# Halving the attention products of chunk 0 in a transformer block, with a new order of work on all engines

## The chip, the cores and the metric

The kernel runs on one core of one Trainium2 chip. A core has a matrix engine (TensorE, PE in the profile), a vector engine (VectorE, DVE), an engine for activations and copies (ScalarE, ACT), a general one (GpSimd, POOL) and one that issues DMAs (SyncE, SP). They run side by side, each through its own list of instructions, and wait for each other by semaphores. Sixteen DMA engines move data for all of them. The metric is the device time of one execution in microseconds (us); less is better.

## The reference

A transformer block on 2048 rows of width 512, in bf16. Attention has 32 heads of width 16; each row looks at 8 earlier rows, 0, 2, ..., 14 back. The MLP has width 1376 and a gated ReLU.

```
qkv = layernorm(x) @ wqkv                    # q, k, v: 32 heads x 16
logits[s, w] = q[s] . k[s - 2*w] * 16**-0.5  # w = 0..7; rows before the first are masked
attn = softmax(logits over w)
o[s] = sum over w of attn[s, w] * v[s - 2*w]
h = x + o @ wo
n = layernorm(h)
out = h + (relu(n @ W_gate) * (n @ W_up)) @ W_down
```

## The kernel before

**Tiling.** The rows are cut into four chunks of 512 (four blocks of 128 rows each). Activations stand transposed in SBUF: the width on the 128 partitions in four tiles (a tile holds 4 of each head's 16 values for all 32 heads), the chunk's 512 rows along the free dimension. kT and vT hold k and v of all rows, so a shift by 2w rows is only another offset.

**The steps of a chunk**, with the names that the code gives them:

- Layer norm of x: statistics on VectorE (`xst`, `xag`, L431, L434), Ln and Exp on ScalarE (L444, L448), the normalised rows on VectorE (`xxn`, L466), then the transposition. It runs on TensorE for chunks 0 to 2 (`xtp`, L495), with copies out of PSUM by ScalarE (`xte`, L511) or VectorE (`xtv`, L509), and by DMA transposes from SyncE for chunk 3 (`xtd`, L484, one for each block of 128 rows).
- Projections (`qkv`, L536): twelve of four matmuls each; the first four of chunk 0 in two halves of the rows (`qka`, `qkc`). ScalarE copies the results to q, kT and vT (`qe`, L544).
- Products q*k (`pr`, L583): one VectorE instruction multiplies two tiles of q by four shifts of k, 128x4096 elements; two for each half of the shifts. TensorE sums them over the head's width by 16 matmuls (`sc`, L589). ScalarE takes the exponentials (`ex`, L619), in chunk 0 VectorE sets the masked ones to zero (`mk`, L622). `den` (L639) forms the denominators, L642 and L645 their reciprocals.
- The weights are spread over the head's width, in chunks 0 and 1 by TensorE (`bc`, L689) and ScalarE's copies (`be`, L695), in chunks 2 and 3 by broadcasting DMAs from SyncE (`bd`, L679).
- Products weight*v (`mu`, L710): one instruction for a tile takes all eight shifts, 128x4096. In chunks 0 to 2 an accumulating DMA that GpSimd issues adds the upper four shifts to the lower four (`ta`, L742, 512 KB each); VectorE adds the rest (`tree`, L713). In chunk 0 the reciprocal denominator is multiplied in at the end (`om`, L717).
- Output projection and residual (`wo`, L762 and L765, with L771 or L773), the second layer norm (L420, L412), its transposition (`htp`, L495 and `hte`, L511, or `htd`, L484), the MLP (`mm`, L800, copies L804 and L807, product `gu`, L820), the down projection (`dn`, L837), the last sum (L848) and the output DMA (`os`, L854).

**What sets the order.** Every step above is registered in a `Plan` with its engine, an assumed duration, the steps it depends on and the buffers it takes. `Plan.order` then simulates the engines: each engine takes its own steps in the order of the table `RANK`, a number for each step, and the buffer that a step gets, and so whom it waits for, follows from that simulated order. The instructions are emitted in the resulting order. TensorE's results share 8 PSUM banks, the products 5 buffers `big`, the MLP products 7 buffers `gT`.

The DMAs of the inputs are issued ahead of the plan, in `setup` (L290 to L321): x of chunk 0, wqk_sb, x of chunk 1, wv_sb, the rest of x, then wo, W_up, W_gate and W_down. 44 warm-up matmuls (L385) and two groups of eight (`fill`, L393) keep TensorE busy until the first weights land.

Of the kernel before, what the change touches and what calls it, by code (L numbers as in the profile page):

```python
# [19 lines left out]
    24, 32, 27, 17, 20, 22, 25, 26, 30, 35, 36, 29, 34, 37, 39, 41, 43, 47, 23, 28,  # L20
    31, 33, 38, 45, 48, 42, 59, 65, 40, 51, 55, 46, 56, 60, 49, 52, 57, 73, 76, 61,
    79, 67, 72, 71, 74, 80, 106, 88, 95, 75, 96, 91, 104, 103, 93, 113, 119, 127, 70, 85,
    94, 98, 102, 172, 175, 185, 130, 134, 136, 149, 152, 105, 108, 110, 114, 111, 188, 197, 223, 226,
    231, 179, 190, 217, 221, 228, 171, 180, 208, 211, 219, 158, 169, 195, 207, 210, 245, 252, 236, 241,
    239, 244, 243, 249, 256, 260, 247, 253, 246, 250, 255, 261, 266, 269, 276, 281, 275, 279, 285, 278,
    283, 282, 286, 291, 310, 315, 326, 330, 293, 322, 314, 324, 348, 329, 361, 337, 345, 339, 342, 346,
    350, 365, 333, 358, 349, 354, 340, 352, 353, 356, 363, 323, 328, 316, 321, 302, 313, 308, 312, 332,
    364, 373, 366, 370, 306, 379, 369, 394, 405, 359, 393, 355, 380, 402, 404, 421, 442, 445, 395, 424,
    453, 574, 374, 413, 447, 450, 389, 409, 436, 473, 50, 53, 44, 62, 54, 64, 58, 63, 66, 69,
    77, 90, 78, 83, 92, 81, 87, 82, 86, 89, 118, 129, 157, 170, 124, 196, 164, 178, 97, 101,  # L30
    166, 182, 100, 116, 150, 159, 132, 186, 107, 176, 137, 156, 109, 126, 200, 213, 218, 237, 232, 240,
    251, 258, 262, 264, 274, 284, 287, 288, 296, 294, 292, 298, 300, 307, 305, 309, 303, 318, 327, 360,
    367, 311, 319, 341, 347, 336, 343, 372, 377, 325, 334, 368, 375, 382, 385, 384, 388, 381, 383, 386,
    398, 390, 392, 397, 400, 387, 396, 401, 403, 406, 407, 408, 411, 414, 417, 410, 418, 412, 419, 422,
    457, 467, 434, 484, 477, 480, 461, 481, 491, 472, 475, 429, 466, 449, 460, 441, 476, 478, 433, 435,
    454, 458, 446, 451, 439, 443, 462, 474, 503, 427, 431, 469, 486, 502, 505, 508, 493, 512, 465, 525,
    507, 518, 511, 521, 529, 497, 516, 504, 513, 520, 531, 552, 569, 572, 524, 541, 666, 707, 514, 533,
    537, 540, 536, 539, 580, 708, 112, 120, 99, 121, 68, 84, 115, 122, 125, 133, 144, 163, 147, 160,
    165, 142, 148, 135, 145, 161, 229, 234, 233, 242, 187, 202, 177, 199, 174, 183, 192, 194, 184, 189,
    206, 235, 212, 215, 181, 191, 193, 205, 214, 238, 289, 265, 297, 317, 248, 257, 290, 301, 331, 335,  # L40
    338, 357, 344, 362, 371, 415, 425, 456, 459, 423, 432, 464, 470, 430, 438, 468, 471, 391, 399, 448,
    455, 479, 483, 490, 495, 485, 492, 482, 488, 487, 489, 499, 501, 494, 496, 498, 506, 509, 515, 519,
    522, 526, 528, 527, 534, 517, 532, 596, 601, 562, 594, 565, 589, 558, 591, 604, 544, 553, 542, 551,
    555, 560, 548, 550, 570, 549, 557, 546, 556, 579, 583, 568, 573, 586, 599, 608, 609, 614, 571, 576,
    603, 611, 618, 617, 626, 613, 629, 588, 631, 606, 627, 632, 620, 624, 585, 616, 635, 639, 662, 668,
    672, 623, 641, 643, 677, 628, 636, 638, 675, 634, 637, 645, 647, 117, 141, 128, 139, 131, 140, 123,
    138, 143, 146, 155, 162, 153, 167, 168, 173, 151, 154, 204, 225, 254, 268, 273, 299, 259, 270, 209,
    227, 216, 220, 267, 280, 224, 230, 201, 222, 198, 203, 263, 272, 271, 277, 304, 295, 320, 376, 378,
    351, 416, 420, 426, 428, 437, 444, 440, 463, 452, 530, 535, 543, 561, 500, 510, 523, 566, 547, 554,
    564, 567, 538, 545, 559, 563, 593, 597, 575, 578, 577, 581, 582, 587, 600, 602, 590, 598, 584, 595,  # L50
    592, 605, 607, 610, 619, 622, 615, 625, 621, 633, 612, 630, 657, 689, 683, 687, 667, 673, 671, 680,
    692, 640, 656, 658, 660, 648, 654, 650, 661, 664, 676, 679, 644, 652, 678, 682, 655, 663, 684, 649,
    651, 653, 670, 642, 646, 665, 669, 674, 694, 696, 685, 693, 659, 690, 681, 686, 698, 691, 699, 688,
    697, 701, 710, 714, 717, 719, 705, 709, 711, 715, 695, 702, 704, 706, 700, 703, 712, 713, 716, 718,
    720, 721,
# [36 lines left out]
class Plan:  # L92


    HOP = 0.06

# [19 lines left out]
    def order(self):  # L116
# [14 lines left out]
        while left:  # L131
# [37 lines left out]
            if op.dq:  # L169
                at = max(t + op.dur + op.dq[0], free.get("DQ", 0.0)) + op.dq[1]  # L170
                free["DQ"] = at
                op.done = at + op.lat
# [19 lines left out]
def kernel(  # L192
# [23 lines left out]
    PRE = ()  # L216
    NAB = 0
# [127 lines left out]
    DAL = 5.5  # L345
    TDD, TDL = 1.25, 1.5
# [13 lines left out]
    HG = ([[0, 1, 2, 3]],) * 4  # L360

# [12 lines left out]
    def load(t):  # L374
        return add(None, "LD", 0.0, None, lat=t)

    xload = [[load(t) for t in (3.5, 3.7, 4.1, 4.35)]] + [[load(t)] * BPC for t in (9.15, 13.2, 15.4)]
    wload = {n: load(t) for n, t in
             (("q", 7.78), ("k", 7.78), ("v", 10.6), ("o", 17.1), ("u", 20.5), ("g", 24.0), ("d", 28.5))}
# [139 lines left out]
    for tk in range(NCK):  # L519
# [49 lines left out]
        for hf in range(2):  # L569
            sc, ex = Buf(at_s), Buf(ex_s)  # L570
            scd, prd = [], []
            for t in range(0, NT, 2):
                pb = Buf(big_s)

                def f_pr(t=t, hf=hf, pb=pb, qT=qT, s0=s0):
                    kb = kT[:, t:t + 2, PADL + s0 - 4 * hf * DIL: PADL + s0 - 4 * hf * DIL + CS]
                    ka = [list(y) for y in kb.ap]
                    k4 = bass.AP(tensor=kb.tensor, offset=kb.offset,
                                 ap=[ka[0], ka[1], [-DIL, 4], ka[2]])
                    qb = qT.t[:, t:t + 2, :]  # L580
                    qa = [list(y) for y in qb.ap]
                    q4 = bass.AP(tensor=qb.tensor, offset=qb.offset, ap=[qa[0], qa[1], [0, 4], qa[2]])
                    V.tensor_tensor(out=pb.t[:].rearrange("p (t w) s -> p t w s", t=2),  # L583
                                    in0=q4, in1=k4, op=ALU.mult)

                def f_sc(t=t, sc=sc, pb=pb):
                    for u in range(2):
                        for g in range(4):
                            nc.tensor.matmul(sc.t[g * HB:(g + 1) * HB, :], lhsT=sel[:],  # L589
                                             rhs=pb.t[:, 4 * u + g, :], start=(t + u == 0),  # L590
                                             stop=(t + u == NT - 1), tile_position=(0, g * HB))

                a = add(("pr%d" % hf, tk), "DVE", D40, f_pr, [d[k] for k in (t, t + 1) for d in (qd, kd, kp)],
                        apr, take=[pb], use=[qT], lat=DL)
                prd.append((a, pb, f_sc))
            if (tk, hf) in PRE:
# [72 lines left out]
        for w0 in range(0, W, BCN):  # L669
            hf = w0 // 4  # L670
            if (tk, hf) in BCD:
                for eng, q in (("SP", nc.sync), ("ACT", nc.scalar), ("POOL", nc.gpsimd)):
# [4 lines left out]
                    def f_bd(ws=ws, q=q, w0=w0, ab=ab, ex=exs[hf]):  # L677
                        for w in ws:
# [3 lines left out]
                                   take=[ab], use=[exs[hf]], lat=0.77, dq=(0.75 - 0.5 * (len(ws) - 1), 0.5 * len(ws))))  # L682
# [19 lines left out]
        for t in range(NT):  # L702
# [13 lines left out]
            def f_om(t=t, mt=mt, rc=rc, OT=OT):  # L716
                V.tensor_tensor(out=OT.t[:, t, :], in0=mt.t[:, 0, :], in1=rc.t[:], op=ALU.mult)  # L717

            m = add(("mu%d" % t, tk), "DVE", D40, f_mu, abd + [vd[t], kdone.get(("v", tk - 1, t))], tpr,
                    take=[mt], use=[ab], lat=DL)  # L720
# [17 lines left out]
            for n, du in ((4, D20), (2, D10), (1, D2)):  # L738
                f = lambda n=n, mt=mt, f=f_a: f(n, mt)
                if n == 4 and (tk, t) in DACC:  # L740
                    def f_da(mt=mt):
                        nc.gpsimd.dma_start(mt.t[:, 0:4, :], mt.t[:, 4:8, :], accum_op=ALU.add)  # L742

                    m = add(("ta%d" % t, tk), "POOL", 1.0, f_da, [m], tpr, use=[mt], lat=1.1, dq=(0.75, 2.74))
                    continue
                if n == 1 and tk in EARLY:
                    oev[t] = add(("tree%d" % t, tk), "DVE", du, f_al, [m], tpr, take=[OT], use=[mt], lat=DL)
                else:
                    m = add(("tree%d" % t, tk), "DVE", du, f, [m], tpr, use=[mt], lat=0.11)
# [39 lines left out]
        for f0 in range(0, NFT, 2):  # L789
# [3 lines left out]
            for ft in fts:  # L793
# [4 lines left out]
                def f_mm(w_sb, mm, ft=ft, fs=fs, hnT=hnT):  # L798
                    for dt in range(NT):
                        nc.tensor.matmul(mm.t[:fs, :], lhsT=w_sb[:, dt, ft * P: ft * P + fs],  # L800
                                         rhs=hnT.t[:, dt, :], start=(dt == 0), stop=(dt == NT - 1))
# [4 lines left out]
                def f_ge(gm=gm, gr=gr, fs=fs, i=ft - f0):  # L806
                    nc.scalar.activation(out=gr.t[:fs, i, :], in_=gm.t[:fs, :], func=ACT.Relu)  # L807

                a = add(("mm%d" % (f0 // 2), tk), "PE", 4 * MM, lambda f=f_mm, um=um: f(wu_sb, um), hev + [wload["u"]], pr,
                        take=[um], use=[hnT], lat=PEL)  # L810
                b = add(("ue%d" % (f0 // 2), tk), "ACT", A5, f_ue, [a], pr - 200, take=[ub], use=[um], lat=AL)
                c = add(("mm%d" % (f0 // 2), tk), "PE", 4 * MM, lambda f=f_mm, gm=gm: f(wg_sb, gm), hev + [wload["g"]], pr,
                        take=[gm], use=[hnT], lat=PEL)
# [93 lines left out]
```

## Time and profile before

| | us |
|---|---|
| median of three runs | 200.72 (200.63 to 201.4) |
| the profiled execution | 201.23 |
| its span, from first to last instruction | 199.5 |
| TensorE busy | 191.6 |
| VectorE busy | 152.6 |
| ScalarE busy | 115.0 |

"Busy" is the time in which an engine has an instruction at work. Matmuls overlap in the array, so their starts say more than their durations: two of 512 columns follow each other after 0.216 us, though one is listed with 0.379 us. The same goes for VectorE, where an instruction starts some 0.08 us before the one ahead of it ends. Between one group's share of busy time and the kernel's time stands the chain of work: the profile follows it back from the last instruction, at each step to what released it. The waits list names for each engine what ended its idle time. A view of the DMA queues gives the packets that each moved in a stretch of time: q1 carries what SyncE issues, q0 what GpSimd issues.

### The profile page before, as it was taken

What the parts mean: (1) busy time and instruction counts of PE and PEld (TensorE: products, weight loads), DVE (VectorE), ACT (ScalarE), POOL (GpSimd) and SP (SyncE); (2) the same over time, 40 slices, a digit from 0 to 9 for tenths busy, and PEclk for the clock granted to TensorE, in tenths of its full rate; (3) what the DMA queues carried; (4) which work ended last, traced back from release to release, by engine and by line L of the source; (5) the groups of instructions that cost most, each with busy time, mean ns of one, the idle gap of its engine ahead of it and who ended that gap; (6) DMA issues with size and microseconds to landing.
All of it is one profiled execution on the core that took longest, in us unless ns stands there. A gap on an engine that the chain in (4) does not pass through costs nothing.

```text
span 199.5 us, 2918 instructions
## 1 busy us (share of the span) xinstructions
PE 191.6 (96%) x1080; PEld 95.7 (48%) x1099; DVE 152.6 (77%) x239; ACT 115.0 (58%) x240; POOL 12.6 (6%) x28
## 2 busy tenths in 40 slices
PE   8599999999999999999999999999999999999994
PEld 8385445554445344444444444444444444444542
DVE  6669999999999999998899859999964423032332
ACT  3455899881999987663844557701439620456500
POOL 4000000330000004100113000000000000000000
PEclk9999999999999999999999999999999999999999
DMA  6959981897000008985269970140010130102022
GB/s 166 327 185 324 412 283 32 156 192 148 3 0 0 3 0 157 190 165 123 39 118 196 208 204 2 26 85 20 3 53 0 26 79 0 31 0 79 0 79 79
DMA packets 19981, 20.92 MB, mean 105 GB/s; under 512 B 8608, under 2 KB 16768, under 8 KB 19968
## 3 DMA queue, kind: packets, MB, share of 16 engines
q1 hardware_dynamic: 17520, 13.60, 23.0%
q0 software_dynamic: 1728, 6.29, 16.8%
q10 hardware_dynamic: 720, 0.85, 1.6%
q8 instruction: 8, 0.13, 0.3%
q14 instruction: 5, 0.04, 0.1%
HBM read 8.42 MB, written 2.10 MB: 53 GB/s over the span
## 4 chain that ended last, share of the span: by engine, by line
PE 91%; DMA 4%; ACT 2%; issue 1%; SPq 1%; DVE 0%
PE bank L800 37%; PE bank L536 21%; PE bank L837 19%; PE bank L762 7%; DMA wqk_sb<-in_A_wqkv_dram 4%; PE bank L589 3%; PE bank L495 2%; ACT big L695 1%; PE bank L639 1%; ACT quad L511 1%; PE bank L765 0%; SPq L292 0%; PE bank L689 0%; ACT quad L544 0%; SPq L294 0%
## 5 line engine op out<-in xcount | busy, mean ns | idle before, releaser
L800 PE MATMUL bank<-quad,wu_sb 128*128 128x512 bf16 (+1 forms) x170 | 42.7, 379 | 0.7 <-ACT quad L511 0.3
L800 PE MATMUL bank<-quad,wg_sb 128*128 128x512 bf16 (+1 forms) x173 | 41.6, 379 | 0.1
L837 PE MATMUL bank<-wd_sb,gT 128*128 128x512 bf16 (+3 forms) x184 | 39.4, 366 | 0.2
L807 ACT ACTIVATE gr<-bank 128x512 bf16<-128x512 f32 (+1 forms) x44 | 25.3, 601 | 23.3 <-PE bank L800 21.8
L804 ACT CAST up_sb<-bank 128x512 bf16<-128x512 f32 (+1 forms) x44 | 25.1, 588 | 23.2 <-PE bank L800 22.4
L710 DVE TENSOR_TENSOR big<-big,vT 128x4096 bf16<-128x4096 bf16 x16 | 36.1, 2290 | 0.8 <-DMA big<-ex 0.6
L583 DVE TENSOR_TENSOR big<-quad,kT 128x4096 bf16<-128x4096 bf16 x16 | 36.2, 2288 | 0.4 <-ACT quad L544 0.4
L536 PE MATMUL bank<-quad,wqk_sb 128*128 128x512 bf16 (+1 forms) x140 | 30.3, 356 | 2.1 <-DMA wqk_sb<-in_A_wqkv_dram 1.8
L820 DVE TENSOR_TENSOR gT<-gr,up_sb 128x1024 bf16<-128x1024 bf16 (+1 forms) x24 | 15.2, 646 | 20.5 <-ACT up_sb L804 10.4
L837 PEld LDWEIGHTS <-gT 128*128 128x128 bf16 (+1 forms) x187 | 18.2, 98 | 19.7
L800 PEld LDWEIGHTS <-wu_sb 128*128 128x128 bf16 (+1 forms) x176 | 17.5, 100 | 21.1 <-issue 1.3
L800 PEld LDWEIGHTS <-wg_sb 128*128 128x128 bf16 (+1 forms) x176 | 17.6, 100 | 20.5 <-issue 0.2
L536 PEld LDWEIGHTS <-wqk_sb 128*128 128x128 bf16 x144 | 15.5, 114 | 14.3 <-DMA wqk_sb<-in_A_wqkv_dram 2.3
L848 DVE TENSOR_TENSOR row<-x_sm,bank 128x512 bf16<-128x512 bf16 (+1 forms) x17 | 10.8, 653 | 10.6 <-PE bank L837 10.6
L713 DVE TENSOR_TENSOR big<-big 128x1024 bf16<-128x1024 bf16 (+2 forms) x24 | 17.2, 735 | 0.7 <-DMA big<-big 0.6
L742 POOL DMA_DIRECT2D big<-big x12 | 10.5, 872 | 86.8 <-DVE big L710 42.7
L536 PE MATMUL bank<-quad,wv_sb 128*128 128x512 bf16 x62 | 15.2, 380 | 0.1
L762 PE MATMUL bank<-wo_sb,quad 128*128 128x512 bf16 x63 | 15.2, 379 | 0.1
L466 DVE TENSOR_SCALAR row<-x_sm,mv,rs 128x512 bf16<-128x512 bf16 x32 | 11.6, 407 | 2.3 <-ACT rs L448 2.1
L431 DVE BATCH_NORM_STATS2 st<-x_sm 128x6 f32<-128x512 bf16 x16 | 10.5, 680 | 3.4 <-DMA x_sm<-in_A_x_dram 3.4
L420 ACT ACTIVATE row<-x_sm,mv 128x512 bf16<-128x512 bf16 x12 | 8.6, 723 | 5.0 <-DVE mv L412 5.0
L544 ACT CAST kT<-bank 128x512 bf16<-128x512 f32 x16 | 9.2, 592 | 3.4 <-PE bank L536 3.4
(68 smaller groups left out, 141.6 us busy)
## 6 DMA issues: line engine op xcount, KB each, us to landing
big<-big POOLq DMA_DIRECT2D x12, 512.0 KB, 5.5
big<-ex SPq DMA_DIRECT2D x16, 128.0 KB, 2.8
out_dram<-row SPq DMA_DIRECT2D x15, 128.0 KB, 1.8
x_sm<-in_A_x_dram SPq DMA_DIRECT2D x3, 512.0 KB, 6.4
wu_sb<-in_B_W_up_dram SPq DMA_DIRECT2D x1, 1376.0 KB, 9.7
wg_sb<-in_B_W_gate_dram SPq DMA_DIRECT2D x1, 1376.0 KB, 12.7
wd_sb<-in_B_W_down_dram SPq DMA_DIRECT2D x1, 1280.0 KB, 15.7
wqk_sb<-in_A_wqkv_dram ACTq DMA_DIRECT2D x2, 256.0 KB, 7.2
```

The source lines that it names most:

```text
L466: V.tensor_scalar(out=xn.t[:], in0=x, scalar1=mv.t[:, j, 0:1], scalar2=rs.t[:, j:j + 1], op0=ALU.add if residual else ALU.subtract, op1=AL ...
L536: nc.tensor.matmul(mm.t[:, lo:hi], lhsT=wv_sb[:, dt, t:D:NT] if c == 2 else wqk_sb[:, dt, c * D + t:(c + 1) * D:NT], rhs=xnT.t[:, dt, lo:h ...
L583: V.tensor_tensor(out=pb.t[:].rearrange("p (t w) s -> p t w s", t=2), in0=q4, in1=k4, op=ALU.mult)
L710: V.tensor_tensor(out=mt.t[:], in0=ab.t[:], in1=v8, op=ALU.mult)
L713: V.tensor_tensor(out=mt.t[:, 0:n, :], in0=mt.t[:, 0:n, :], in1=mt.t[:, n:2 * n, :], op=ALU.add)
L762: nc.tensor.matmul(od.t[:], lhsT=OT.t[:, t, j * P:(j + 1) * P], rhs=wo_sb[:, t, :], start=(t == 0), stop=(t == NT - 1 and tk not in RPE))
L800: nc.tensor.matmul(mm.t[:fs, :], lhsT=w_sb[:, dt, ft * P: ft * P + fs], rhs=hnT.t[:, dt, :], start=(dt == 0), stop=(dt == NT - 1))
L804: nc.scalar.copy(out=ub.t[:fs, i, :], in_=um.t[:fs, :])
L807: nc.scalar.activation(out=gr.t[:fs, i, :], in_=gm.t[:fs, :], func=ACT.Relu)
L820: V.tensor_tensor(out=gt.t[:fs, 0:n, :], in0=gr.t[:fs, 0:n, :], in1=ub.t[:fs, 0:n, :], op=ALU.mult)
L837: nc.tensor.matmul(od.t[:, c0:c1], lhsT=gts[ft].t[:fs, ft % 2, j * P:(j + 1) * P], rhs=wd_sb[:fs, ft, c0:c1], start=(ft == 0), stop=(ft == ...
L848: V.tensor_tensor(out=ob.t[:, c0:c1], in0=x_sm[:, tk * BPC + j, c0:c1], in1=od.t[:, c0:c1], op=ALU.add)
```

## The change

In chunk 0 alone (`PRS`, `MUH`), each q*k product is cut by tile (`pr..a` for the first tile of the pair, `pr..c` for the second), so that the first half needs q and k of one tile only; and each weight*v product is cut by halves of the shifts (`mu..a` for shifts 0 to 3, `mu..c` for 4 to 7), so that a half needs the four spread weights of its half only. The matmuls that sum the scores still wait for all the products of their half of the shifts, the accumulating DMA for both halves of its tile. The plan has 8 steps more for that, and the whole table `RANK` is another one, so the order changes on every engine.

The plan's assumptions also change: the inputs are assumed to land 0.8 to 1.0 us later, and a DMA that SyncE or ScalarE issues beside one of GpSimd's is assumed to move on at a share of 0.18. Three new options (`PRD`, `DAC2`, `HSP`) are off. The input DMAs, the matmuls and their shapes stay as they are.

```diff
+    SHARE = 0.18
...
-                at = max(t + op.dur + op.dq[0], free.get("DQ", 0.0)) + op.dq[1]
-                free["DQ"] = at
+                at, sw, busy = t + op.dur + op.dq[0], free.get("DQ", 0.0), op.dq[1]
+                if op.eng == "POOL":
+                    at = free["DQ"] = max(at, sw) + busy
+                else:
+                    at = max(at, free.get("DQ" + op.eng, 0.0))
+                    late = max(sw - at, 0.0)
+                    at += busy / self.SHARE if late * self.SHARE >= busy else late + busy - late * self.SHARE
+                    free["DQ" + op.eng] = at
...
-    xload = [[load(t) for t in (3.5, 3.7, 4.1, 4.35)]] + [[load(t)] * BPC for t in (9.15, 13.2, 15.4)]
+    xload = [[load(t) for t in (3.5, 3.7, 4.1, 4.35)]] + [[load(t)] * BPC for t in (10.0, 14.0, 16.2)]
...
+                if tk in PRS:
+                    def f_p1(u, t=t, hf=hf, pb=pb, qT=qT, s0=s0):
+                        kb = kT[:, t + u, PADL + s0 - 4 * hf * DIL: PADL + s0 - 4 * hf * DIL + CS]
...
+                        V.tensor_tensor(out=pb.t[:, 4 * u:4 * u + 4, :],
+                                        in0=qT.t[:, t + u, :].unsqueeze(1).to_broadcast([P, 4, CS]), in1=k4, op=ALU.mult)
+
+                    for u in range(2):
+                        a = add(("pr%d%s" % (hf, "ac"[u]), tk), "DVE", D20, lambda u=u, f=f_p1: f(u),
+                                [d[t + u] for d in (qd, kd, kp)], apr, take=[pb], use=[qT], lat=DL)
+                        prd.append((a, pb, f_sc if u else lambda: None))
...
+            if tk in MUH:
+                def f_m1(hf, t=t, ab=ab, mt=mt, s0=s0):
...
+                    V.tensor_tensor(out=mt.t[:, 4 * hf:4 * hf + 4, :], in0=ab.t[:, 4 * hf:4 * hf + 4, :], in1=v4, op=ALU.mult)
+
+                ms = [add(("mu%d%s" % (t, "ac"[hf]), tk), "DVE", D20, lambda hf=hf, f=f_m1: f(hf),
+                          [x for x in abd if x.key[0][2] == str(hf)] + vds, tpr, take=[mt], use=[ab], lat=DL) for hf in range(2)]
+            else:
+                ms = [add(("mu%d" % t, tk), "DVE", D40, f_mu, abd + vds, tpr, take=[mt], use=[ab], lat=DL)]
```

The order before and after, as the instructions are issued, at the places where it differs most (@0 is chunk 0; a number behind a name is the block, tile or projection; an a or c behind it a half):

```
TensorE, start      before  xtp0 xtp1 fill fill qka1 qka0 xtp2 xtp3 qka2 qka3 qkc1 qkc3 qkc2 qkc0 ...
                    after   xtp0 fill xtp1 fill xtp3 qka3 xtp2 qka1 qka0 qka2 qkc0 qkc1 qkc2 ...
VectorE, chunk 0    before  pr1 xxn@1 x4 pr1 pr0 ... pr0 ... xxn@2, xxn@3 x3 mu3 xxn@3 mu2 mu1 mu0
                    after   pr1a xxn@1 x4 pr1c pr1a pr1c pr0a pr0c pr0a pr0c ... mu3c ... mu3a ...
                            mu2c mu2a mu1a xxn@3 x4 mu1c mu0c mu0a
TensorE, first use of chunk 3's rows
                    before  behind 27 whole projections of chunks 0 to 2
                    after   behind 32 of them
TensorE, first MLP  before  htp htp htp htp bc0@1 sc1@2 mm@0 sc0@2 bc1@1 mm@0 ...
                    after   htp htp qkv1@3 htp htp bc0@1 sc1@2 mm@0 sc0@2 bc1@1 mm@0 ...
```

## The prediction

> **What bounds the kernel now.** I read the page's busy shares and its chain of work first, then TensorE's waits.
>
> ```profile
> PE 191.6 (96%) x1080; PEld 95.7 (48%) x1099; DVE 152.6 (77%) x239; ACT 115.0 (58%) x240; POOL 12.6 (6%) x28
> ...
> PE 91%; DMA 4%; ACT 2%; issue 1%; SPq 1%; DVE 0%
> ...
> PE bank L536 <- DMA wqk_sb<-in_A_wqkv_dram: 1.8, 2, 1.0
> PE bank L385 <- DVE warm L297: 1.0, 1, 1.0
> PE bank L495 <- DVE row L466: 0.5, 1, 0.5
> PE bank L800 <- ACT quad L511: 0.3, 1, 0.3
> ```
>
> TensorE is the chain. Behind the first weights (10.05 us) one wait is listed, 0.3 us. TensorE issues as many matmuls after the change as before, in the same shapes, so the change can give back only the little that TensorE still idles, and whatever makes TensorE wait anew is added in full. The clock row shows 9 in every slice, so the clock is left out.
>
> **What the new order removes.** Four pieces, from the trace's matmul starts (512 columns are 0.216 us apart, so a projection of four takes 0.863 us).
> 1. While it waited for wqk_sb, TensorE before had nothing queued; block 2's and block 3's transposes (L495, 0.22 us each) came behind the first two half projections, at 10.73 us. Now block 3's stands ahead of them, in the idle time: 0.22 us.
> 2. The first second-half projection before started 0.17 us late, because VectorE's copy of block 3 (L509) ended at 12.17 us. Now that copy comes before 9 us: 0.17 us.
> 3. At 66.45 us the first MLP matmul waited for ScalarE's second copy of the transposed rows (L511): a gap of 0.43 us, where such a switch behind L589 costs 0.10 us elsewhere. Now a projection (0.86 us) stands between the two pairs of transposes, so the first copy (these start 0.91 us apart) runs beside it: 0.33 us.
> 4. At 69.05 us the second MLP group waited for a bank behind ScalarE's L695 and L544: 0.27 us where 0.10 us is usual. With point 3 ScalarE starts these copies earlier against TensorE: 0.17 us.
> Sum: 0.9 us. What is late next at points 3 and 4 has 0.2 to 0.3 us to spare by ScalarE's spacing (0.48 us a copy).
>
> **What the split costs.** Eight 128x4096 products become sixteen of 128x2048.
>
> ```profile
> L583 DVE TENSOR_TENSOR big<-quad,kT 128x4096 bf16<-128x4096 bf16 x16 | 36.2, 2288 | 0.4 <-ACT quad L544 0.4
> L710 DVE TENSOR_TENSOR big<-big,vT 128x4096 bf16<-128x4096 bf16 x16 | 36.1, 2290 | 0.8 <-DMA big<-ex 0.6 <-issue 0.2
> ...
> L713 DVE TENSOR_TENSOR big<-big 128x2048 bf16<-128x2048 bf16 x4 | 4.9, 1222 | 0.1
> ```
>
> Back to back the first two start 2.20 us apart, the third 1.134 us before its successor, so a split costs 0.07 us and eight 0.5 us. VectorE is not on the chain. It also starts sooner: the first product needs only q and k of tile 0, ready at about 13.6 us (before, both tiles, 15.35 us). Summing VectorE's new order from the landing of chunk 1's x (11.15 us): four L431 and four L434 to 13.8, then eight halves of q*k and eight of weight*v at 1.134 us, twelve L466 at 0.32, eight L431 at 0.59, ten small ones at 0.07: 27.5 us, so the last product of chunk 0 ends at 41.4 us, before 42.1. That 0.6 us gained covers the cost. From there to the last output product it was 10.1 us, 0.4 of them a wait for q that is gone: 51.1 us (before 52.2). The wo projection that needs it stands at 53.39 - 0.86 (one projection fewer ahead of it) - 0.39 (points 1 and 2) = 52.1 us: 1.0 us to spare, before 1.2. If this cover were gone, the split would cost at most its 0.5 us.
>
> **What is moved, and the wait it adds.** Chunk 3's rows are transposed by SyncE's DMAs (L484), not by TensorE. Before, three of chunk 3's normalised rows (L466) came ahead of the first weight*v product, and the first transpose was issued at 32.18 us. Now all four come behind the first half of the third one: by the same sum at 36.8 to 38.1 us, so the four issues run from 37.2 to 42.4 us (5.23 us, as before). There they meet POOL's accumulating DMAs (L742). These follow the products' ends (now 32.3, 35.6, 39.3, 41.4 us) by 0.3 to 0.6 us to issue and 1.4 us more to the first packet; one takes 2.7 us of all 16 DMA engines (512 KB at the 197 GB/s of 41 to 42 us). So the second moves at 37.5 to 40.3, the third at 41.2 to 44.0, the fourth right behind it, to 46.8 us.
>
> What happens to a transpose there, the last one of before shows. The DMA queues at 36 to 37 us (transposes alone), at 37.6 to 40 us (beside the first accumulating DMA) and at 40.4 to 41 us (that one ending):
>
> ```profile
> q1 hardware_dynamic: 544, 0.13, 65.1%
> ...
> q0 software_dynamic: 112, 0.46, 107.1%
> q1 hardware_dynamic: 103, 0.03, 8.5%
> ...
> q1 hardware_dynamic: 381, 0.09, 72.0%
> q0 software_dynamic: 24, 0.07, 66.1%
> ...
> DMA to landing us min/median/max: 2.5/2.5/5.3
> ```
>
> q1 carries the transposes, 512 packets of 256 bytes each; q0 the accumulating DMA, 4096 bytes a packet. Alone q1 moved 544 packets in a microsecond; beside q0 103 in 2.4 us, 43 a microsecond, about one for each big packet; once q0 stopped, 635 a microsecond (367 in 0.4 us at 101.8 to 102.2, 918). That transpose landed after 5.3 us instead of 2.5. At 100.7 to 101.5 us, beside another accumulating DMA, q1 moved none at all.
>
> The four transposes are 2048 packets, the first at 38.05 us (0.85 us behind the issue, as before). Beside the second DMA to 40.3: about 100. In the pause to 41.2: 0.9 us at 800 a microsecond, 700. Beside the third and fourth (5.9 us with what they are slowed): 250. Left at 47.0 us: 1000, at 800 a microsecond 1.25 us, 0.15 us for the landing: 48.4 us.
>
> When does TensorE want them? Before, eight projections stood between the first of chunk 3 and the scores at 49.53 us: it began at 42.63 us, 1.6 us behind the last transpose (41.0 us). Now 32 whole projections stand ahead of it instead of 27: 42.63 + 5 x 0.863 - 0.39 (points 1 and 2) = 46.55 us. **The wait is 48.4 - 46.55, 1.9 us.** Queued behind that projection on TensorE are four more of chunk 3, chunk 1's scores and wo, so nothing fills it. Bounds: no wait, if the transposes land by 46.5; 2.8 us, if the pause gives nothing (700 packets more behind the fourth DMA, 0.9 us). I take 1.9, nearest to the 43 a microsecond row. It isn't given back: all later steps hang on TensorE, whose spare time there only grows.
>
> [...]
>
> **Sum.** The profiled execution took 201.23 us (span 199.5, 1.7 around it), 0.5 above the median 200.72. 201.23 - 0.9 + 1.9 (2.0 with the restart of TensorE's pipeline) = 202.3; on the median **201.8 us**, 0.55% slower.
>
> Of the other issues, eight warm-up matmuls move between the first two transposes, into idle time; on SyncE chunk 3's weight broadcasts now go ahead of all of chunk 0's output rows and chunk 3's second transposes ahead of chunk 1's outputs, each waiting for its own rows only.
>
> **The later stages** I walked with the same spacings, up to the last block: the nearest are 0.2 us (ScalarE's and VectorE's bank releases at about 67 and 175 us), 0.7 us (wo of chunk 1) and 0.6 us (chunk 1's down projection). Wherever a row is that close the estimate could fail; each failure costs some tenths. The tail is the same: half a row block, its sum, its DMA, 3.2 us behind the last matmul.
>
> **Rivals.**
> - *The queue drains whenever an accumulating DMA ends* (ends not slower). For: the 381 in 0.6 us, all that was left, went between two such DMAs, and the next began only as they ended. If 1100 go likewise at 44 us, they land at 45.6 us, before 46.55: no wait, 200.72 - 0.9 = 199.8 us. Against: the pause of before was 0.4 us, 320 packets at 800. It decides from 1050 packets on. Chance 0.23.
> - [...] Chance 0.12.
> - *A second wait of this kind*: chunk 1's two transposes meet the accumulating DMA of chunk 2 (at about 98 to 101 us), and chunk 3's weight broadcasts (L679) meet all three of that chunk; their spare time is 0.8 us in my sum. Or the early gains don't come, the change not doing what it says. 0.7 to 1 us more: 202.7 us. Chance 0.15.
> - The forecast: 0.50, by itself 201.2 to 202.7 us.
>
> **How the numbers follow.** Half a percent, 1.0 us, is about what a measurement of this kernel tells from no change. The first two rivals (0.35) lie at 199.8, 0.1 us inside that bound: faster 0.14, same 0.21. The forecast gives 0.18 to same (waits below 1.9 us) and 0.32 to slower, the third rival 0.15 to slower. Together 0.14, 0.39, 0.47. The range takes in both ends of the wait: 199.6 to 203.0 us.
>
> **What would show it.** In TensorE's waits, L536's successor waiting for DMA quad<-row at about 46.5 us, 1.9 us long, and landing times of 4 to 8 us for those transposes: right. [...] No wait at 66 us for ScalarE's L511: point 3 right. VectorE's last chunk 0 product ending near 41.4 us: the sum of the split right. A wait at 100 us, or at chunk 3's first weight*v product: the third rival. What would make it wrong most likely is the share that the transposes get, of which before has two short stretches.

## The result and the profile after

208.94 us (median of four, 208.35 to 209.92) against 200.68 us: 1.0413 times before, interval 1.0374 to 1.0451. That is 8 us slower, where 1.1 us were forecast. The profiled execution took 209.19 us, its span is 207.4 us (before 199.5). All ratios here leave out executions that took over 1.5% more than the fastest of their kernel. From the page, the lines of TensorE, of its granted clock in 40 slices of 5.19 us, and of the chain by engine:

```profile
PE 196.1 (95%) x1099; PEld 96.0 (46%) x1099; DVE 152.9 (74%) x247; ACT 116.4 (56%) x240; POOL 12.8 (6%) x28
...
PEclk9999999997599999999999999999999999999999
...
PE 57%; DVE 18%; DMA 12%; ACT 6%; SPq 3%; issue 2%; DVEq 0%; ACTq 0%
```

The clock has two slices below 9, at 52 us; the mean granted clock of the four executions is 0.981 to 0.984. The chain, 91% TensorE's before, now runs through VectorE, DMAs and SyncE's queue. TensorE's waits say where:

```profile
PE bank L547 <- DMA quad<-row: 4.5, 1, 4.5
PE bank L547 <- DMA wqk_sb<-in_A_wqkv_dram: 1.0, 1, 1.0
PE bank L902 <- DVE gT L885: 1.0, 1, 1.0
...
PE bank L857 <- DMA quad<-row: 0.3, 1, 0.3
```

(The projections are L536 before and L547 after, the MLP L857, the down projection L902, the product `gu` L885.) The first line is the wait that was forecast, chunk 3's first projection for its transposes: TensorE has nothing to do from 46.00 to 50.65 us. The 0.3 us of L511 at the first MLP matmul are gone. The last two lines, at 133 and 110 us, are new.

**The wait.** What SyncE's queue did, after and then before (start, time, line, count):

```profile
36.59 9.61 SPq L495 DMA_TRANSPOSE quad<-row  x4
```

```profile
32.18 5.23 SPq L484 DMA_TRANSPOSE quad<-row  x4
```

The same four issues took 9.6 us instead of 5.2. And the transposes were long under way; the answer for after, from issue to landing (before 2.5/2.5/5.3):

```profile
DMA to landing us min/median/max: 5.5/7.7/9.5
```

The DMA queues of after beside the second accumulating DMA (37.2 to 40.3 us), in the pause behind it (40.3 to 40.9), beside the third (41 to 46) and the fourth (46 to 49.6); packets, MB, share of the 16 engines' time:

```profile
q0 software_dynamic: 142, 0.52, 95.6%
q1 hardware_dynamic: 189, 0.05, 7.4%
...
q1 hardware_dynamic: 553, 0.13, 108.1%
...
q0 software_dynamic: 137, 0.52, 89.1%
q1 hardware_dynamic: 586, 0.14, 35.5%
...
q0 software_dynamic: 145, 0.51, 72.2%
q1 hardware_dynamic: 631, 0.15, 20.9%
```

q1, the transposes, got 61 packets a microsecond beside the second, 117 and 175 beside the others: more than the 43 that I took. But each slows the other: the first accumulating DMA, ahead of them, moved from 33.89 to 36.64 us, 2.76 us; the third, among them, from 40.92 to 46.98, 6.06 us. The last accumulating DMA ended at 49.65 us, the last transpose landed at 50.5.

**The clock.** Behind the wait the matmuls of 512 columns start 0.427 us apart instead of 0.216. The stretches of a microsecond of after around it (behind the comma PE's busy time comes first; the granted clock is the third number from the end):

```profile
49.00:50.00 1.00, 0.00 (x0) 0.00 (x0) 0.00 (x0) 0.00 (x0) 0.00 (x0) 0.74 0.68 142
50.00:51.00 1.00, 0.35 (x1) 0.15 (x2) 0.97 (x3) 0.00 (x0) 0.00 (x0) 0.50 0.01 1
...
55.00:56.00 1.00, 1.00 (x4) 0.33 (x3) 1.00 (x1) 0.83 (x2) 0.00 (x0) 0.50 0.00 0
56.00:57.00 1.00, 1.00 (x5) 0.48 (x4) 0.47 (x1) 0.00 (x0) 0.00 (x0) 0.84 0.00 0
```

The clock fell to half at 49.48 us (0.74 of that microsecond), in the idle time, and rose at 56.3. From 50.65 to 56.3 TensorE did half as much: 2.8 us lost, on top of the wait.

**The later waits.** At 133.1 us the down projection of chunk 1 has a gap of 1.16 us (0.09 is usual there): it needs `gu`, which stands on VectorE behind chunk 2's sums and chunk 3's first weight*v product. VectorE's waits of after:

```profile
DVE big L753 <- DMA big<-big: 2.9, 2, 1.7
...
DVE big L750 <- DMA out_dram<-row: 0.8, 1, 0.8
```

The first are the sums behind accumulating DMAs, 1.7 us of it chunk 2's. The second is that product; out_dram is only what came last by the profile, the product needs SyncE's eight broadcasts (L718). They were issued beside three accumulating DMAs in 10.96 us from 110.93 on; before, beside one, in 7.17 us from 110.34 (after, then before):

```profile
110.93 10.96 SPq L718 DMA_DIRECT2D big<-ex  x8
```

```profile
110.34 7.17 SPq L679 DMA_DIRECT2D big<-ex  x8
```

At 110.0 us the MLP of chunk 1 waited 0.47 us for chunk 1's transposes, beside another one. Both causes are read from the trace, not isolated by a run.

**Sum.** 4.6 (the wait over the usual gap) + 2.8 (clock) + 1.1 + 0.4 (the later waits over theirs) = 8.9 us. The span grew by 7.9, so 1.0 us came in, 0.53 of it because the first weights came at 9.52 instead of 10.05 us in this execution.

### The profile page after: what moved, and what is told of

It is laid out like the page before. It is cut to its first block, busy times and chain, and to the rows that moved or that the text cites. A ratio compares the mean times of both kernels' runs of the same rounds, so it can differ in the third digit from the quotient of the medians.

```text
span 207.4 us, 2959 instructions
## 1 busy us (share of the span) xinstructions
PE 196.1 (95%) x1099; PEld 96.0 (46%) x1099; DVE 152.9 (74%) x247; ACT 116.4 (56%) x240; POOL 12.8 (6%) x28
## 3 DMA queue, kind: packets, MB, share of 16 engines
q1 hardware_dynamic: 17520, 13.60, 22.7%
## 4 chain that ended last, share of the span: by engine, by line
PE 57%; DVE 18%; DMA 12%; ACT 6%; SPq 3%; issue 2%; DVEq 0%; ACTq 0%
PE bank L857 33%; PE bank L902 15%; DMA quad<-row 6%; PE bank L819 5%; DMA x_sm<-in_A_x_dram 5%; DVE big L609 4%; PE bank L547 4%; DVE st L442 3%; DVE row L477 3%; SPq L495 3%; DVE big L765 3%; DVE big L750 2%; DVE x_sm L830 2%; DMA out_dram<-row 1%; ACT row L431 1%
## 5 line engine op out<-in xcount | busy, mean ns | idle before, releaser
L857 PE MATMUL bank<-quad,wg_sb 128*128 128x512 bf16 (+1 forms) x176 | 42.9, 379 | 0.3 <-DMA quad<-row 0.3
L857 PE MATMUL bank<-quad,wu_sb 128*128 128x512 bf16 (+1 forms) x176 | 42.9, 379 | 0.1
L902 PE MATMUL bank<-wd_sb,gT 128*128 128x512 bf16 (+3 forms) x187 | 40.2, 367 | 1.0 <-DVE gT L885 1.0
L547 PE MATMUL bank<-quad,wqk_sb 128*128 128x512 bf16 (+1 forms) x144 | 32.8, 370 | 5.5 <-DMA quad<-row 4.5
L885 DVE TENSOR_TENSOR gT<-gr,up_sb 128x1024 bf16<-128x1024 bf16 (+1 forms) x24 | 15.3, 643 | 28.1 <-issue 11.0
L902 PEld LDWEIGHTS <-gT 128*128 128x128 bf16 (+1 forms) x187 | 18.1, 98 | 21.4 <-DVE gT L885 1.5
L750 DVE TENSOR_TENSOR big<-big,vT 128x4096 bf16<-128x4096 bf16 x12 | 27.2, 2285 | 1.1 <-DMA out_dram<-row 0.8
L594 DVE TENSOR_TENSOR big<-quad,kT 128x4096 bf16<-128x4096 bf16 x12 | 27.1, 2285 | 0.2 <-ACT kT L555 0.2
L857 PEld LDWEIGHTS <-wg_sb 128*128 128x128 bf16 (+1 forms) x176 | 17.4, 100 | 21.1 <-DMA quad<-row 0.8
L857 PEld LDWEIGHTS <-wu_sb 128*128 128x128 bf16 (+1 forms) x176 | 17.5, 100 | 20.7 <-issue 0.7
L547 PEld LDWEIGHTS <-wqk_sb 128*128 128x128 bf16 x144 | 15.7, 115 | 18.4 <-issue 7.7
L753 DVE TENSOR_TENSOR big<-big 128x1024 bf16<-128x1024 bf16 (+2 forms) x24 | 16.7, 731 | 3.0 <-DMA big<-big 2.9
L547 PE MATMUL bank<-quad,wv_sb 128*128 128x512 bf16 x64 | 17.5, 401 | 0.0
L555 ACT CAST vT<-bank 128x512 bf16<-128x512 f32 x16 | 9.2, 600 | 7.6 <-PE bank L547 7.6
```

The source lines that it names most:

```text
L547: nc.tensor.matmul(mm.t[:, lo:hi], lhsT=wv_sb[:, dt, t:D:NT] if c == 2 else wqk_sb[:, dt, c * D + t:(c + 1) * D:NT], rhs=xnT.t[:, dt, lo:h ...
L750: V.tensor_tensor(out=mt.t[:], in0=ab.t[:], in1=v8, op=ALU.mult)
L753: V.tensor_tensor(out=mt.t[:, 0:n, :], in0=mt.t[:, 0:n, :], in1=mt.t[:, n:2 * n, :], op=ALU.add)
L857: nc.tensor.matmul(mm.t[:fs, lo:hi], lhsT=w_sb[:, dt, ft * P: ft * P + fs], rhs=hnT.t[:, dt, lo:hi], start=(dt == 0), stop=(dt == NT - 1))
L885: V.tensor_tensor(out=gt.t[:fs, 0:n, :], in0=gr.t[:fs, 0:n, :], in1=ub.t[:fs, 0:n, :], op=ALU.mult)
L902: nc.tensor.matmul(od.t[:, c0:c1], lhsT=gts[ft].t[:fs, ft % 2, j * P:(j + 1) * P], rhs=wd_sb[:fs, ft, c0:c1], start=(ft == 0), stop=(ft == ...
```

## The experiments

My theory by then: the place of chunk 3's rows on VectorE sends the transposes among the accumulating DMAs; that makes TensorE idle; idle TensorE gets half the clock; two smaller waits of the same kind come later. Rivals: the split makes the loss; the clock falls for another reason; the transposes are late only because they are issued late.

Where a step is moved, the table of numbers gets an exception:

```diff
-            op.prio = RANK[op.seq]
+            op.prio = SET.get((key, sum(o.key == key for o in self.ops)), RANK[op.seq])
```

### Is it the split?

**The split alone** (`e5_before_split`): the new code with the old table and assumptions, each half's number directly behind the other's.

> The split alone: the kernel before with its own order, chunk 0's eight products cut into sixteen halves that stand where the whole ones stood, the two halves of one behind each other. Theory (the split itself costs TensorE nothing; its 0.07 us a product, 0.5 us in all, lies in VectorE's spare time, and half of it is given back since the first half needs one tile only): 200.4 to 201.0 us, within 0.5% of before. Rival (the split costs what it adds on VectorE, or its halves delay the accumulating DMAs): 201.1 to 201.5 us, up to all of the 8 us if it were the cause of the change's loss.

200.82 us, 0.9997 of before (0.9971 to 1.0023). The transposes are issued from 32.09 us in 5.23 us, as before. The split costs nothing that can be measured.

**The order without the split** (`e7_after_merged`):

```diff
-    PRS, MUH = (0,), (0,)
+    PRS, MUH = (), ()
```

> The changed kernel's order without the split: each pair of halves is one whole product again, where the pair's later half stood (chunk 3's rows stay ahead of the product of tile 1). Theory (the order makes the loss, the split has no part in it): the transposes of chunk 3 are issued at 37 us again, meet the accumulating DMAs, TensorE waits 4 us or more at its 46 us point and the clock falls behind it: 207 to 210 us. Rival (the split makes the loss): 202 us or less.

207.62 us, 1.0336 (1.0274 to 1.0398). The wait is there, a little shorter, and in the profiled execution (209.16 us) the clock is lost as well: its mean is 0.982 (after 0.981), and a matmul behind the wait is listed with 0.591 us where 0.379 is usual:

```profile
PE bank L547 <- DMA quad<-row: 3.6, 1, 3.6
```

The order makes the loss. The executions differ in it: the mean clock of the other three is 0.992, 1.000 and 0.992, and the one with full clock took 206.08 us; how long TensorE waited in these three isn't traced. The later gaps (0.47 at 110.3, 1.10 at 133.2 us) are those of after too.

### Is it where chunk 3's rows stand?

**Rows early in the changed kernel** (`e3_rows_early`):

```diff
+SET = {
+    (('xst', 3), 0): 138, (('xxn', 2), 3): 144.1,
+    (('xag', 3), 0): 145.3, (('xag', 3), 2): 145.2, (('xag', 3), 3): 145.1,
+    (('xrl', 3), 0): 156.1, (('xre', 3), 0): 156.2,
+    (('xxn', 3), 0): 157.4, (('xxn', 3), 1): 157.2, (('xxn', 3), 2): 157.1, (('xxn', 3), 3): 157.3,
+}
```

> The changed kernel, split and all, with chunk 3's rows alone moved back to an early place: its statistics and normalised rows come ahead of the second half product of the second tile (mu2c), some 3 us earlier, so that the four transposes are issued from about 33.7 us instead of 36.6. Theory (where the rows stand is the cause): the last transpose lands by 46 us, the wait of 4.5 us and the slow clock behind it go, 4.6 + 2.7 = 7.3 us less, at most 0.5 us of wait left: 201.6 to 202.1 us; the later waits of 0.5 and 1.2 us (at 110 and 133 us of the changed kernel) stay. Rival (the split or the other moves cost it): above 205 us.

202.53 us, 1.0104 (1.0031 to 1.0178); the clock stays full (1.000 in all four executions). 6.4 us of the loss are gone with this one step. A wait of 1.0 us stays, twice what I allowed, and the issues still took 8.6 us:

```profile
PE bank L562 <- DMA quad<-row: 1.0, 1, 1.0
```

```profile
32.45 8.60 SPq L510 DMA_TRANSPOSE quad<-row  x4
```

They begin at 32.45 us, as before (32.18), and yet take 3.3 to 8.3 us to land (before 2.5 to 5.3), as among accumulating DMAs. In after, with the same halves of products, the first of these moved from 33.89 us (before 37.35), since the products ahead of it end earlier. So in this order, as I read it, the earlier products bring the collision forward. Two gaps of 0.5 and 0.3 us behind VectorE (at wo and the down projection) stay as well.

**Rows late in the kernel before** (`e9_before_rows_late`), nothing else changed:

```diff
+SET = {(('xxn', 3), 0): 179.1, (('xxn', 3), 1): 179.2, (('xxn', 3), 2): 179.3, (('xxn', 3), 3): 179.4}
```

> The opposite transplant: the kernel before, no split, with one step moved: chunk 3's four normalised rows come behind chunk 0's product of tile 1 on VectorE, ahead of the last, as in the changed kernel. Theory (this place alone is enough to make the loss): the transposes are issued from about 38 us, meet the last three accumulating DMAs, and land 1 us behind the last of them, at 47 to 50 us; TensorE, which wants them at 42.6 us, waits 5 to 7 us, the clock falls behind it for 3.4 to 6.8 us (1.7 to 2.8 us more): 207 to 211 us. Rival (the loss needs the earlier products of the split as well): a wait under 2 us, 203 us or less.

212.69 us, 1.0593 (1.0549 to 1.0638), more than I expected. This one step makes a wait of twice the length, and three slices of slow clock (the clock row of its page, then TensorE's first wait):

```profile
PEclk9999999985699999999999999999999999999999
```

```profile
PE bank L544 <- DMA quad<-row: 9.3, 1, 9.3
```

SyncE's issues ran from 40.20 us for 9.32 us; TensorE wanted the rows at 42.1 and got them at 51.6. The place of the rows is enough to make the loss, and in the changed kernel taking it back removes most of it. But this run is not the changed kernel's case over again: TensorE wants the rows 4 us earlier and they are issued 3.6 us later. Alone, by the spacing of before (the fourth issue starts 4.0 us behind the first, landing 2.5 us later), they would land at 46.7 us, an estimate; so about half of the 9.5 us is lateness and half the collision. In after the same estimate gives 43.1 us, ahead of 46.0: there nothing would have waited.

### Is it the accumulating DMAs, or only the late issue?

**Two of the four on VectorE** (`e4_adds_on_dve`); the rows stay late:

```diff
-    DACC = tuple((k, t) for k in range(3) for t in range(4))
+    DACC = tuple((k, t) for k in range(3) for t in range(4) if k or t > 1)
```

> The changed kernel with two of chunk 0's four accumulating DMAs (tiles 1 and 0, the last two) replaced by VectorE additions of 1.13 us each; the rows of chunk 3 and the issues of their transposes stay where they were. Theory (the transposes are late because they share the queues with the accumulating DMAs): beside one of them only, the transposes land by 44 us, no wait, no slow clock: 201.6 us, plus nothing for VectorE's 2.3 us since the additions replace a wait of VectorE for these DMAs. Rival (the transposes are late because they are issued late, whatever moves beside them): a wait of 3 us or more stays, 206 us or more.

The transposes were issued from 36.40 us, as late as in after, in 6.6 us (first line), and landed after the times of the second:

```profile
36.40 6.60 SPq L495 DMA_TRANSPOSE quad<-row  x4
```

```profile
DMA to landing us min/median/max: 2.5/2.8/4.7
```

TensorE's wait for them is gone, and so is the slow clock (1.000 in all four executions): the accumulating DMAs were what made them late. But the time is 204.31 us, 1.0173 (1.0116 to 1.0231), 2.7 us more than I expected:

```profile
PE bank L819 <- DVE quad L757: 1.5, 1, 1.5
PE bank L819 <- DVE quad L787: 1.1, 1, 1.1
```

VectorE's two additions were not free: wo of chunk 0 now waits 1.5 us for its last output product (the first line), and the denominators of chunk 1 wait 0.8 us for the exponentials. The second line is wo of chunk 2 at 118.6 us, beside the broadcasts.

### Does idle time cost the clock?

**Keeping TensorE busy** (`e1_keep_busy`; `e2_half_busy` with 36):

```diff
-            def f_mm(lo=0, hi=CS, c=c, t=t, mm=mm, xnT=xnT):
+            def f_mm(lo=0, hi=CS, c=c, t=t, mm=mm, xnT=xnT, busy=72 if (tk, n) == (3, 4) else 0):
+                for _ in range(busy):
+                    nc.tensor.matmul(mm.t[:, 0:P], lhsT=warm[:], rhs=warm[:], start=True, stop=True)
```

> The changed kernel with 72 warm-up matmuls of 128 columns (zeros, 0.056 us each, 4.0 us) put ahead of chunk 3's first projection, into the bank that it takes. The wait for the transposes stays, only TensorE isn't idle in it. Theory (the idle time makes the clock fall, the slow clock costs 2.7 us of its own): the landing stays at about 50.6 us, the matmuls behind it start 0.216 us apart instead of 0.427, the clock row shows 9 throughout, and the time falls by 2.7 us to 206.2. Rival (the clock falls for another reason, such as the DMA traffic, or matmuls of zeros don't count): still 0.427 us apart, 208.9.

At this place as the theory has it: 1.05 us of idle time left, the projection at 50.4 us, full clock behind it, and the stretch from there to the second MLP group takes 22.0 us instead of 24.8. The ratio doesn't show it: 1.0322 (1.0221 to 1.0424), single executions from 206.39 to 211.88 us. The one with a full clock (0.999) is the 206.39 us, where 206.2 was expected; the others have 0.992, 0.984 and 0.992, and the rest of their spread isn't traced. In the profiled one the later wait of 110 us had grown to 2.14 us, and the clock fell behind that (TensorE's first wait, then stretches as above):

```profile
PE bank L859 <- DMA quad<-row: 2.0, 1, 2.0
```

```profile
109.00:110.00 1.00, 0.88 (x4) 0.46 (x5) 1.00 (x2) 0.00 (x0) 0.00 (x0) 0.85 0.94 159
110.00:111.00 1.00, 1.00 (x4) 0.29 (x2) 1.00 (x1) 0.00 (x0) 0.00 (x0) 0.50 0.99 158
...
113.00:114.00 1.00, 1.00 (x6) 0.39 (x4) 1.00 (x3) 0.69 (x2) 0.00 (x0) 0.94 0.89 159
```

> The same with 36 of these matmuls, 2.0 us, so that about 2.6 us of TensorE's 4.66 us of idle time stay. Theory in its strong form (any stretch without matmuls of this order makes the clock fall): as the changed kernel, 208.9 us, or a shorter slow stretch in proportion to the idle time. [...]

1.0285 (1.0168 to 1.0401), single executions from 205.18 to 213.31 us. In the profiled one the transposes landed 2 us later, so that 4.8 us of idle time stayed behind the 36 matmuls, and the clock fell at 50.17 us, 2.26 us into them. The time doesn't answer the question it was built for, whether 2.6 us are enough; the 2.14 us above do. The execution with a full clock (1.000) took 205.18 us.

**The same where nothing waits later** (`e12_late_rows_busy`): the kernel before with late rows, and `busy=160 if (tk, n) == (3, 9)`.

> The kernel before with chunk 3's rows late (its run had a wait of 9.5 us at 42.1 us, the clock at half from 46.2 to 56.4 us, and 212.7 us) and 160 warm-up matmuls of zeros (9.0 us) ahead of the waiting projection, so that TensorE isn't idle while it waits. Nothing else waits later in this kernel, so the clock's share shows in the time. Theory (idle TensorE makes the clock fall, and the half clock cost 51.6 to 56.4 us, 2.4 us of it, on top of the wait): the transposes land at about 51.5 us as before, the clock row shows 9 throughout, 210.3 us. Rival (the slow matmuls come from the transfers or the zeros don't count): 212.7 us.

The landing is at 52.3 us, later by 0.65, and the clock stays full (the page's clock row, then the wait that is left):

```profile
PEclk9999999999999999999999999999999999999999
```

```profile
PE bank L546 <- DMA quad<-row: 0.9, 1, 0.9
```

210.74 us, 1.0503 (1.0474 to 1.0531) against 1.0593 without the matmuls: 1.9 us less by doing more, 2.4 expected, and the later landing is what is missing. The mean clock is 1.000 in all four executions, 0.974 to 0.976 without the matmuls. So here the idle time itself cost the clock, and matmuls of zeros prevented it; the same transfers move beside both (SyncE's issues take 9.55 us, there 9.32).

### The later waits

**Broadcasts behind the outputs again** (`e8_rows_and_broadcasts`): rows early, and

```diff
+    (('bd1S', 3), 0): 467.5, (('bd0S', 3), 0): 467.6,
```

> The changed kernel with chunk 3's rows early (as in the run of that kind) and with chunk 3's weight broadcasts behind the first two output DMAs of chunk 0 on SyncE again, as before the change. Theory (these eight broadcasts, issued from 104.5 us, run beside three accumulating DMAs of chunk 2 and slow the last of them; VectorE's sum waits 2.3 us for it and TensorE's wo 0.6 us): the sum's wait goes, and with it the gap of 0.62 us at wo, 201.9 us. Rival (the broadcasts are now what is late: chunk 3's first weight*v product stands on VectorE ahead of rows and MLP products that TensorE wants): the gap moves behind that product and grows to 1 to 2 us, 203 us or more.

205.55 us, 1.0226 (1.018 to 1.0273): the rival. The gap at wo is gone, but 0.67 us at 126.6 and 1.54 us at 128.1 stand in its place, and in the profiled execution (206.22 us) the clock fell for 3.4 us behind them. Four others have a mean clock of 0.998 to 1.000 and took 204.41 to 205.63 us, so most of the loss of this run is the waits.

```profile
PE bank L919 <- DVE gT L902: 1.4, 1, 1.4
```

In this order VectorE's MLP products stand behind the product that needs the broadcasts, so late ones cost TensorE; early ones run beside the accumulating DMAs (their issues take 10.68 us in `e3_rows_early`, 7.17 in before). Neither of the two places tried is free.

### The gains by themselves

**Points 1 and 2 on the kernel before** (`e6_before_moves`):

```diff
+SET = {(('xtp3', 0), 0): 39.1, (('xtp2', 0), 0): 39.2, (('xtv3', 0), 0): 43.5}
```

> The early gains alone: the kernel before, no split, with three steps moved: the transposes of blocks 3 and 2 of chunk 0 ahead of the first half projection, where TensorE waits for wqk_sb, and VectorE's copy of them ahead of chunk 1's first statistics. Theory (points 1 and 2 of the prediction are real and the change lost them under its waits): 0.22 to 0.44 us for the transposes and 0.17 for the copy, 0.4 to 0.6 us less than before in the same runs, 200.0 us. Rival (given back later at another wait, since all of TensorE's later waits are set by VectorE or DMAs): no change, 200.5.

200.21 against 200.62 us, 0.9989 (0.9968 to 1.001). The waits for wqk_sb and for the copy are gone from TensorE's list, but at 17.73 us it now waits 0.36 us for chunk 1's rows: most of the gain is given back there.

**With the split and those rows earlier** (`e10_split_and_moves`: numbers 70.1 to 70.4 for `xxn` of chunk 1):

> The parts that cost nothing together: the kernel before with the split in place, the two early transposes and the early copy moved as in the run of the moves alone, and chunk 1's four normalised rows between the first two halves of the q*k products, where the whole product kept TensorE waiting 0.36 us at 17.7 us. Theory: 0.4 us from the moves and 0.25 us from these rows, no new wait: 0.5 to 0.7 us less than before in the same runs, 199.9 us. Rival (the earlier halves shift the accumulating DMAs onto the transposes again, or the rows only move the wait): 200.5 us or more.

200.49 us, 1.0001 (0.9981 to 1.0021). The gap of 17.7 us is gone, a wait of 0.52 us for VectorE's masked exponentials at 23.3 us has come: the rival, only moved.

**With one projection ahead of the transposes instead** (`e11_moves_and_one`: `(('qkv9', 0), 0): 82`):

> The kernel before, no split, with the early transposes and the early copy as in the run of the moves alone, and one projection more: chunk 0's v projection of tile 1 stands ahead of all four transposes of chunk 1 instead of three of them, which filled TensorE's new gap of 0.36 us at 17.7 us. Theory: 0.4 us as in that run and the 0.36 us it gave back there: 199.8 us, 0.3 to 0.45% faster than before, by which it would beat both kernels. Rival (ScalarE's copies of these transposes come 0.9 us later and chunk 1's first projection or chunk 0's scores wait for them, so the gap only moves): 200.2 to 200.6 us.

200.17 us against 200.43, 0.9983 (0.9968 to 0.9997): the best of all, faster than both kernels by the interval, though only by 0.17%, half of what I expected, and barely clear of 1 as one of a dozen comparisons. 0.42 us came back at 22.7 us:

```profile
PE bank L697 <- DVE ex L630: 0.3, 1, 0.3
```

## Why the prediction was wrong, point by point

- **Points 1 and 2: the size was right.** TensorE reached the place of the wait at 46.00 us. I had 46.55, and the first weights came 0.53 us earlier. On the kernel before most of it came back as another wait (0.11% in place of 0.2 to 0.3).
- **Point 3: right.** The switch at 72.9 us costs 0.10 us. **Point 4: wrong**, the gap is still 0.25 us.
- **The split: right.** VectorE's last product of chunk 0 ended at 40.94 us (41.4 forecast); alone the split is 0.9997.
- **The added wait: right place and cause, wrong size, 4.6 us for 1.9.** Two terms of the sum failed, and the last transpose landed at 50.5 us for 48.4. "The four issues run from 37.2 to 42.4 us (5.23 us, as before)": they ran from 36.6 to 46.2, since SyncE's issues slow down too. And the accumulating DMAs at "2.7 us" each: the third took 6.06, the fourth 3.73. I let the transposes suffer from them and allowed only 0.5 us for the reverse (5.9 us for two). The trace of before had hints of both: SyncE's eight broadcasts took 5.21 us at 85.9 us, where the last accumulating DMA of a chunk was ending, and 7.17 at 110.3, beside one; and the accumulating DMA beside the last transpose moved from 37.35 to 40.64 us, 3.3 us. The share of 43 packets a microsecond was too low (61 to 175), the pause shorter (0.6 us, 553 packets, for 0.9 and 700); these errors partly cancel. Even my upper bound, 2.8 us, kept both terms as they were. The 0.1 us for a restart of TensorE's pipeline was an estimate that no run shows: behind the wait of after four matmuls started in 1.67 us, the next four in 1.71.
- **"The clock is left out": the third term that failed, 2.8 us put at nothing.** I read the row of 9s as a property of the kernel. The runs show it only for a TensorE that is kept busy: idle for 9.5 us it had a mean clock of 0.974 to 0.976 (`e9_before_rows_late`), with matmuls of zeros in that wait 1.000 (`e12_late_rows_busy`), and I was adding idle time. At the 1.9 us that I forecast it was a close call (1.83 us in `e8_rows_and_broadcasts` left the clock full, 2.14 in `e1_keep_busy` didn't, see the end); with the wait of after the mean clock was 0.981 to 0.984 in all four executions. The slow stretches last 6.84 us (after), 3.42 (`e1_keep_busy`) and 10.2 (`e9_before_rows_late`). TensorE was at work in 5.7, 3.4 and 4.8 us of them, at half the clock, so they cost 2.8, 1.7 and 2.4 us on top of the wait. What sets their length, no run shows.
- **The rivals.** The first two, which had the transposes land in time, are out. The third, a second wait of this kind, came in addition: 0.4 us at 110 us and 1.1 at 133. I had priced it as an alternative, 0.7 to 1 us, where, as the trace reads, the same mechanism that makes the first wait made both.

The range ended at 203.0 us. The wait's excess (2.7 us), the clock (2.8) and the later waits (1.5) are 7.0 us, about what lies between 201.8 and 208.9. Of the 2.7 us, 2.1 are the late landing; the rest is TensorE's earlier arrival, gained at the start and lost again here, so some half a microsecond of the difference stays unassigned.

## What to carry to other kernels

A transfer moved among others is priced by when all of them are done: here its own issues (9.61 us for 5.23), its packets (landed after 7.7 us for 2.5, the medians) and a transfer beside it (6.06 us for 2.76) all slowed down. A wait on TensorE can cost its length and a slow clock behind it, as 4.65 us did in after (2.8 us more) and 2.14 in `e1_keep_busy` (1.7), so a full clock row says nothing of a schedule with a new wait. And an order in which one engine has less than a microsecond to spare gave early gains back at the next place (0.36 us at 17.73 us in `e6_before_moves`): look there before counting them.

## What the runs showed of the hardware

- **How little idle time the clock fell behind.** In `e1_keep_busy` TensorE was idle from 106.98 to 109.12 us, 2.14 us, and the clock fell at 109.70, 0.58 us after TensorE had taken up work. It fell 2.26 us into 4.8 us of idle time in `e2_half_busy` (50.17 us), 3.5 us into 4.65 in after (49.48) and 4.1 us into 9.5 in `e9_before_rows_late` (46.2). In `e8_rows_and_broadcasts` it fell at 129.88 us behind two pieces, 0.67 and 1.54 us, with 0.8 us of work between them; 1.83 us in one piece at 45.55 left it full in the same execution, as 1.16 us did in after. So of the single pieces the longest that left it full had 1.83 us and the shortest that it fell behind 2.14; but the two pieces of `e8_rows_and_broadcasts`, each shorter, show that the length of one piece doesn't decide alone. What does, no run shows.
- **It doesn't rise at once.** In after TensorE was busy again from 50.65 us, and the clock rose at 56.3, 5.7 us later; in `e1_keep_busy` 4.0 us later (109.12, 113.1).
- **SyncE's issue itself slows.** Four transposes: 5.23 us in before (1.20 to 1.31 each), where the first accumulating DMA began to move at 37.35 us, in the last of them; 6.60 in `e4_adds_on_dve` with two of chunk 0's four accumulating DMAs left; 8.04 (`e7_after_merged`) to 9.61 (after, 1.84 to 2.90 each) with all four.
